# Two small weight loads moved onto the main load queue, and block diagonals built on VectorE instead of TensorE

## The chip, the cores and the metric

The kernel runs on one core of one Trainium2 chip. The metric is the device time of one execution in microseconds (us). Executions are in one of two states, fast or slow. The profile records one execution; its span is some 2 us shorter than the time quoted for the same execution.

Names used below: PE is TensorE, PEld its weight load, DVE is VectorE, ACT is ScalarE, POOL is GpSimd, SP is SyncE. SPq and ACTq are lines of the profile for the sequencers of SP and ACT issuing DMAs.

## The reference, cut to what matters

The function is a gated mix of a linear attention and a gated feed-forward block over 2048 tokens of width 640. The change touches only the front of the attention branch: the per-head 20x20 weights w_phi, and the vector gate_w.

```python
g  = sigmoid((x * gate_w).sum(-1, keepdims=True))
qkv = x @ wqkv                                   # 640 -> 3 * 640, 32 heads of 20
pq = einsum("bhsd,hdf->bhsf", q, w_phi)          # per head 20 x 20
pk = einsum("bhsd,hdf->bhsf", k, w_phi)
# softmaxes of +-pq and +-pk, linear attention, @ wo  -> a ; geglu ffn -> b
return g * a + (1 - g) * b
```

The kernel folds w_phi into the k and q weights: it multiplies a transposed weight matrix by a block diagonal matrix made of w_phi ("fold"). So the first fold needs two things, the block diagonals (`BD`) and the transposed k weights (`wkT`). gate_w becomes one more column behind the folded k weights (`w3[:, :, 2*D]`), so that one projection computes k and the gate together.

## The kernel before

The loads stand in this order. SP issues nearly everything; x of block 0 and the v weights come as plain loads, the rest of x and the k and q weights as transposing loads. ACT issues the two small loads.

```python
sc.dma("act", wphi_sb[20 partitions, (h f)] <- w_phi "h d f -> d h f")     # 25 KB, 640 pieces of 40 bytes
sc.dma("act", gw_row[1, 640] <- gate_w)                                    # one row
xload(0); xload(2)                                # SP: x of block 0, two halves
for kt in range(KD): vload(kt)                    # SP: v weights, five pieces
xblock(1)                                         # SP, transposing: x of block 1 -> xT
wload(wkT, D, "wkT"); wload(wqT, 0, "wqT")        # SP, transposing: k, then q weights
xblock(2); xblock(3)
# ... feed-forward weights ...
```

PE then makes the block diagonals and the gate column with ten small matmuls, and DVE masks them out of PSUM:

```python
# blockdiag(): five matmuls spread w_phi (20 partitions) over 128 partitions by a selection matrix,
# five 1x1 matmuls turn the gate row into a column; then, for i in 0..4:
DVE tensor_tensor: BD[:, i] = psum * mask[:, i]   # 0 outside the diagonal blocks
DVE tensor_copy:   w3[:, :, 2*D] = gate column
```

The order of work on PE at the front is:

```python
warm(7)                                  # matmuls on zeros while x is on its way
xt(0..3)                                 # 20 PE transposes of x of block 0
vs(...)                                  # v of token tiles 0..3, the block diagonals in between
self.v_early(4, 6); self.v_early(5, 0)   # v of tiles 4, 5: need x of block 1
f(0, "k", ...); f(1, "k", ...)           # folds: need BD and wkT
self.v_early(6, 6)
f(2, "k", ...); f(3, "k", ...); f(4, "k", ...)
...
```

The softmax here doesn't subtract the row's maximum and nothing guards it: scores larger than these inputs give would overflow.

## Time and profile before

| | |
|---|---|
| time, median (range of 6 runs) | 299.75 us (299.39 to 300.2) |
| span of the profiled run | 297.8 us |
| PE busy | 292.9 us, 98% |
| PE on the chain that ended last | 96% |

The page of the kernel before: its span; the busy time of each engine (us, share, number of instructions); and the chain that ended last, first by engine, then by source line.

```profile
span 297.8 us, 4821 instructions
...
PE 292.9 (98%) x1913; PEld 171.9 (58%) x1913; DVE 162.2 (54%) x318; ACT 104.3 (35%) x183; POOL 29.0 (10%) x58
...
PE 96%; DMA 1%; ACT 1%; issue 0%; SPq 0%; ACTq 0%
PE ps L616 37%; PE ps L694 20%; PE ps L359 13%; PE ps L700 7%; PE ps L504 7%; PE ps L649 4%; PE ps L452 3%; PE ps L368 2%; PE ps L626 1%; DMA xtok<-in_A_x_dram 1%; PE ps L339 1%; ACT Eq L510 1%; ACT Ek L418 0%; PE ps L284 0%; PE ps L304 0%
```

PE is busy 98% of the span and is 96% of the chain: whatever the change does, it shows only if it removes PE work or makes PE wait. Line L616 is the feed-forward matmul; nothing of the change is near it.

The front of the same execution, from the view of instructions in order of time. Columns: start in us, length in us, engine, source line, operation, output<-inputs, shape, count, and in brackets the idle time before it and what ended that.

```profile
4.19 3.83 SPq L229 DMA_TRANSPOSE xT<-in_A_x_dram  x1
...
4.40 0.73 PE L284 MATMUL ps<-ident,xtok 128*128 128x128 bf16 x10
...
5.45 0.73 PE L284 MATMUL ps<-ident,xtok 128*128 128x128 bf16 x10 [0.32 <-DMA xtok<-in_A_x_dram]
...
8.06 3.35 SPq L226 DMA_TRANSPOSE wkT<-in_A_wqkv_dram  x1
...
9.39 0.48 PE L304 MATMUL ps<-wphi_sb,esel 20*128 20x140 bf16 x5
...
9.71 0.26 PE L312 MATMUL ps<-one,gw_row 1*128 1x1 bf16 x5
...
12.10 2.88 PE L359 MATMUL ps<-w,xT 128*128 128x512 bf16 x20
...
14.99 0.80 PE L339 MATMUL ps<-BD,wkT 128*128 128x140 bf16 x12
```

Read it in two columns. PE: ten transposes of x at 4.40, a wait of 0.32 us for the second half of x, ten more at 5.45, the ten small matmuls at 9.39 and 9.71, v of tiles 4 and 5 at 12.10, and the first fold at 14.99. SP: the transposing load of x of block 1 is issued from 4.19 for 3.83 us, that of the k weights from 8.06 for 3.35 us. The trace has the last of the k weights landing at 14.95 us, and PE begins the fold at 14.99 without having idled.

### The profile page before, as it was taken

To read this page: it belongs to the slowest core of one execution; us is meant where nothing else is said; L and a number is where in the kernel's file an instruction comes from. 1 tells how busy PE (TensorE), PEld (TensorE's weight loads), DVE (VectorE), ACT (ScalarE), POOL (GpSimd) and SP (SyncE) were. 2 spreads that over 40 slices of the span, in tenths; PEclk is the share of its full clock that TensorE was granted. 3 is DMA by queue.
4 is the path that set the end of the run, shared out by engine and by line. 5 is a ranking of instruction groups with operands and counts; after the bars stand their busy time and mean duration, and the time that the engine had idled before them with its cause. 6 is when DMAs were issued, how large, how long until landed. Compare 5 with 4: busy or idle time off the path is not lost.

```text
span 297.8 us, 4821 instructions
## 1 busy us (share of the span) xinstructions
PE 292.9 (98%) x1913; PEld 171.9 (58%) x1913; DVE 162.2 (54%) x318; ACT 104.3 (35%) x183; POOL 29.0 (10%) x58
## 2 busy tenths in 40 slices
PE   7999999999999999999999999999999999999996
PEld 3576656555544556775555577655457765545763
DVE  1348999998875679514655700455580045567000
ACT  3367787576663221121222212122221212232111
POOL 7000000000000011201011100101110010111000
PEclk9999999999999999999999999999999999999999
DMA  7999990000002122112011200201101010110101
GB/s 219 211 209 335 355 350 18 0 0 2 0 2 53 35 20 28 47 44 66 3 22 22 20 27 24 60 6 25 22 9 37 22 46 23 22 24 0 44 24 44
DMA packets 38098, 18.77 MB, mean 63 GB/s; under 512 B 30203, under 2 KB 37820, under 8 KB 38076
## 3 DMA queue, kind: packets, MB, share of 16 engines
q1 hardware_dynamic: 37424, 18.44, 24.4%
q8 instruction: 15, 0.25, 0.3%
q10 hardware_dynamic: 652, 0.03, 0.1%
q14 instruction: 7, 0.06, 0.1%
HBM read 8.96 MB, written 2.62 MB: 39 GB/s over the span
## 4 chain that ended last, share of the span: by engine, by line
PE 96%; DMA 1%; ACT 1%; issue 0%; SPq 0%; ACTq 0%
PE ps L616 37%; PE ps L694 20%; PE ps L359 13%; PE ps L700 7%; PE ps L504 7%; PE ps L649 4%; PE ps L452 3%; PE ps L368 2%; PE ps L626 1%; DMA xtok<-in_A_x_dram 1%; PE ps L339 1%; ACT Eq L510 1%; ACT Ek L418 0%; PE ps L284 0%; PE ps L304 0%
## 5 line engine op out<-in xcount | busy, mean ns | idle before, releaser
L616 PE MATMUL ps<-xT,wu_sb 128*128 128x512 bf16 x260 | 64.6, 379 | 0.2 <-ACT Eq L510 0.2
L616 PE MATMUL ps<-xT,wg_sb 128*128 128x512 bf16 x260 | 64.6, 379 | 0.0
L694 PE MATMUL ps<-wd_sb,hT 128*128 128x320 bf16 (+2 forms) x448 | 63.6, 299 | 0.0
L621 DVE TENSOR_TENSOR hT<-ps,gl 128x512 bf16<-128x512 f32 x52 | 35.7, 688 | 44.5 <-PE ps L616 44.4
L619 ACT ACTIVATE gl<-ps 128x512 bf16<-128x512 f32 x52 | 31.1, 597 | 80.8 <-PE ps L616 78.6
L694 PEld LDWEIGHTS ps<-wd_sb,hT 128*128 128x128 bf16 x448 | 43.2, 98 | 17.8
L616 PEld LDWEIGHTS ps<-xT,wu_sb 128*128 128x128 bf16 x260 | 25.4, 98 | 31.1 <-issue 0.7
L359 PE MATMUL ps<-w,xT 128*128 128x512 bf16 (+3 forms) x240 | 40.9, 321 | 0.0
L616 PEld LDWEIGHTS ps<-xT,wg_sb 128*128 128x128 bf16 x260 | 25.0, 98 | 27.2
L710 ACT ACTIVATE outsb<-ps,Gm 128x640 bf16<-128x640 f32 (+2 forms) x17 | 13.0, 763 | 74.7 <-PE ps L700 74.7
L678 POOL TENSOR_TENSOR Og<-O,O 128x640 bf16<-128x640 bf16 x16 | 22.3, 1394 | 167.5 <-DVE O L676 167.5
L359 PEld LDWEIGHTS ps<-w,xT 128*128 128x128 bf16 x240 | 22.4, 97 | 18.2
L665 DVE RECIPROCAL RH<-ps 128x32 f32<-128x32 f32 x16 | 5.7, 358 | 40.7 <-PE ps L649 39.7
L429 DVE TENSOR_REDUCE Dk<-Ek 128x64 f32<-128x1280 bf16 x16 | 23.7, 1480 | 3.2 <-ACT gcol L421 3.2
L438 DVE TENSOR_TENSOR Ek<-Ek,Dk 128x640 bf16<-128x640 bf16 x32 | 25.0, 821 | 0.6
L504 PE MATMUL ps<-xT,wq 128*128 128x512 bf16 x100 | 24.7, 379 | 0.3 <-ACT Eq L510 0.3
L676 DVE TENSOR_TENSOR O<-ps,RH 128x640 bf16<-128x640 f32 x32 | 24.8, 816 | 0.0
L700 PE MATMUL ps<-wo_sb,goT 128*128 128x320 bf16 (+2 forms) x160 | 24.5, 299 | 0.0
L510 ACT ACTIVATE Eq<-ps 128x512 bf16<-128x512 f32 x40 | 21.7, 604 | 4.0 <-PE ps L504 4.0
L418 ACT ACTIVATE Ek<-ps 128x640 bf16<-128x640 f32 x32 | 20.7, 702 | 3.5 <-PE ps L359 3.5
L700 PEld LDWEIGHTS ps<-wo_sb,goT 128*128 128x128 bf16 x160 | 15.5, 98 | 6.3
L649 PEld LDWEIGHTS ps<-KV,Eq 128*128 128x128 bf16 x192 | 12.0, 98 | 3.1
(66 smaller groups left out, 154.2 us busy)
## 6 DMA issues: line engine op xcount, KB each, us to landing
out_dram<-outsb SPq DMA_DIRECT2D x15, 160.0 KB, 2.0
wd_sb<-in_B_w_down_dram SPq DMA_DIRECT2D x1, 2080.0 KB, 12.4
wg_sb<-in_B_w_gate_dram SPq DMA_DIRECT2D x1, 1120.0 KB, 5.7
wu_sb<-in_B_w_up_dram SPq DMA_DIRECT2D x1, 1120.0 KB, 9.6
wg_sb<-in_B_w_gate_dram SPq DMA_DIRECT2D x1, 960.0 KB, 9.9
wu_sb<-in_B_w_up_dram SPq DMA_DIRECT2D x1, 960.0 KB, 10.2
w<-in_A_wqkv_dram SPq DMA_DIRECT2D x5, 160.0 KB, 4.0
wo_sb<-in_A_wo_dram SPq DMA_DIRECT2D x1, 800.0 KB, 10.1
```

The lines of the kernel that those rows point to most:

```text
L359: sc.op("pe", lambda e, kt=kt: e.matmul(self.bank(bank)[:, bcol:bcol + n], self.xT[:, kt, t * P:(t + 1) * P], self.w3[:, kt, c0:c0 + n], s ...
L429: sc.op("dve", lambda e: e.tensor_reduce(self.Dk[:, se, 0, :].rearrange("p (s h) -> p s h", h=H), self.Ek[:, se, :, :].rearrange("p s (h d ...
L438: sc.op("dve", lambda e, v=v, r=r: e.tensor_tensor(v, v, r, ALU.mult), reads=[("Rk", se)], writes=[("Ek", se, s)])
L504: sc.op("pe", lambda e, kt=kt: e.matmul(self.bank(bank), self.wq2[:, kt, i * P:(i + 1) * P], self.xT[:, kt, b * self.BT:(b + 1) * self.BT] ...
L510: sc.op("act", lambda e, s=s, scale=scale: e.activation(self.Eq[:, s, i, b * self.BT:(b + 1) * self.BT], self.bank(bank), AF.Exp, scale=sc ...
L616: sc.op("pe", lambda e, kt=kt, w=w, bk=bk: e.matmul(self.bank(bk), w[:, kt, c * P:(c + 1) * P], xs(kt), start=(kt == 0), stop=(kt == self. ...
L619: sc.op("act", lambda e: e.activation(self.gl[:, slot, :], self.bank(banks[0]), AF.Gelu_apprx_tanh), reads=[("ps", banks[0])], writes=[("g ...
L621: sc.op("dve", lambda e: e.tensor_tensor(self.hT[:, c, :], self.bank(banks[1]), self.gl[:, slot, :], ALU.mult), reads=[("ps", banks[1]), ( ...
L649: sc.op("pe", lambda e, s=s, i=i, n=n, o0=o0, k0=k0, bk=bk, r=r: e.matmul(self.bank(bk)[:, o0:o0 + n], self.Eq[:, s, i, t * P:(t + 1) * P] ...
L676: dve(lambda e, o=o, f=f, s=s: e.tensor_tensor(o, V[s][:, :, :, 0:DH], f, ALU.mult), rb + [key(6 + s)], [("O", s, sl)], guard=old)
L694: sc.op("pe", lambda e: e.matmul(self.bank(bk, w), self.hT[:, c, tt * P:(tt + 1) * P], self.wd_sb[:, c, w0:w0 + w], start=(c == 0), stop=F ...
L700: sc.op("pe", lambda e: e.matmul(self.bank(bk, w), self.goT[:, gs, k, :], self.wo_sb[:, k, w0:w0 + w], start=False, stop=(k == self.KD - 1 ...
```

## The change

The intent is to free PE of ten small matmuls and to bring x in sooner. w_phi is loaded so that each of its 640 features stands on its own partition; the block diagonal is then one product of a broadcast and a mask. The gate weights are loaded straight into their column, one element per partition and row. Both loads now stand on SP behind v, and the second half of x of block 0 goes to ACT's queue.

```diff
+        xload("sp", 0)
+        xload("act", 2)
         for kt in range(KD):
             sc.dma("sp", ... self.w3[:, kt, 0:D] <- v weights ...)
-        sc.dma("act", ... self.wphi_sb[20 partitions] <- "h d f -> d h f" ...)
-        sc.dma("act", ... self.gw_row[0:1, :] <- gate_w ...)
-        xload(0); xload(2)                                        # both on SP
+        sc.dma("sp", lambda e: e.dma_start(
+            self.wphi_sb[:, :, :], self.wphi.rearrange("h d f -> (h d) f").rearrange("(i p) f -> p i f", p=P)), ...)
+        sc.dma("sp", lambda e: e.dma_start(
+            self.w3[:, :, 2 * D:2 * D + 1], self.gw.rearrange("(k p o) -> p k o", p=P, o=1),
+            allow_slow_non_contiguous=True), ...)
 ...
-    def blockdiag(self, banks):     # 10 matmuls, 5 products from PSUM, 1 copy
+    def blockdiag(self):
+        for i in range(self.KD):
+            n = self.HHI[i] - self.HLO[i] + 1
+            self.sc.op("dve", lambda e: e.tensor_tensor(
+                self.BD[:, i, 0:n * DH].rearrange("p (h d) -> p h d", d=DH),
+                self.wphi_sb[:, i, :].unsqueeze(1).to_broadcast([P, n, DH]),
+                self.mask[:, i, 0:n].unsqueeze(2).to_broadcast([P, n, DH]), ALU.mult), ...)
 ...
-        vs(0,0) vs(1,0) vs(2,0) vs(0,1) vs(3,0) vs(1,1) vs(2,1) vs(3,1)
+        for t in range(4): vs(t, 0)
+        for t in range(4): vs(t, 1)
```

More of the change, by code (lines that the diff above doesn't have):

```diff
@@ L156, in alloc @@
         self.zero = T("zero", [P, 512], BF16)
-        self.gw_row = T("gw_row", [1, D], BF16)
-        self.one = T("one", [1, 1], BF16)
         self.gcol = T("gcol", [P, NT], F32)
@@ L163, in alloc @@
         self.BD = T("BD", [P, KD, 8 * DH], BF16)
-        self.wphi_sb = T("wphi_sb", [DH, D], BF16)
-        self.esel = T("esel", [DH, 8, DH], BF16)
+        self.wphi_sb = T("wphi_sb", [P, KD, DH], BF16)
         def place(lists):
@@ L209, in loads, with xload @@
         x4 = self.x[0:self.BT, :].rearrange("(p j) n -> p j n", j=self.TB)
-        def xload(j):
-            sc.dma("sp", lambda e: e.dma_start(self.xtok[:, j:j + 2, :], x4[:, j:j + 2, :]),
+        def xload(q, j):
+            sc.dma(q, lambda e: e.dma_start(self.xtok[:, j:j + 2, :], x4[:, j:j + 2, :]),
                    writes=[("xtok", j), ("xtok", j + 1)])
-        def vload(kt):
+        xload("sp", 0)
+        xload("act", 2)
+        for kt in range(KD):
             sc.dma("sp", lambda e: e.dma_start(self.w3[:, kt, 0:D], w3[:, kt, 2 * D:3 * D]), writes=[("wv", kt)])
-        sc.dma("act", lambda e: e.dma_start(self.wphi_sb[:, :].rearrange("d (h f) -> d h f", f=DH),
-                                            self.wphi.rearrange("h d f -> d h f")), writes=["wphi"])
-        sc.dma("act", lambda e: e.dma_start(self.gw_row[0:1, :], self.gw.rearrange("(o n) -> o n", o=1)), writes=["gw_row"])
-        xload(0)
-        xload(2)
-        for kt in range(KD):
-            vload(kt)
+        sc.dma("sp", lambda e: e.dma_start(
+            self.wphi_sb[:, :, :], self.wphi.rearrange("h d f -> (h d) f").rearrange("(i p) f -> p i f", p=P)),
+            writes=["wphi"])
+        sc.dma("sp", lambda e: e.dma_start(
+            self.w3[:, :, 2 * D:2 * D + 1], self.gw.rearrange("(k p o) -> p k o", p=P, o=1),
+            allow_slow_non_contiguous=True), writes=["wgate"])
         def wload(T, c0, key):
@@ L257, in loads @@
                                        compare_op=ALU.not_equal, fill=1.0, base=0, channel_multiplier=1), ["ident"])
-        pool(lambda e: e.tensor_copy(
-            self.esel[:, :, :], self.ident[0:DH, 0:DH].unsqueeze(1).to_broadcast([DH, 8, DH])), ["esel"], reads=["ident"])
         for i in range(KD):
@@ L292, in x_transpose @@
             sc.op("dve", lambda e: e.tensor_copy(out, src), reads=[("ps", b)], writes=[("xT", t)])
-    def blockdiag(self, banks):
-        sc = self.sc
+    def blockdiag(self):
         DH = self.DH
-        es = self.esel[:, :, :].rearrange("d j f -> d (j f)")
-        plan = []
-        for bk, chunks in zip(banks, ((0, 1, 2), (3, 4))):
-            c = 0
-            for r, i in enumerate(chunks):
-                n = (self.HHI[i] - self.HLO[i] + 1) * DH
-                off = (P * i) % DH
-                sc.op("pe", lambda e, i=i, n=n, c=c, off=off, bk=bk, r=r: e.matmul(
-                    self.bank(bk)[:, c:c + n], es[:, off:off + P],
-                    self.wphi_sb[:, self.HLO[i] * DH:self.HLO[i] * DH + n], start=(r == 0), stop=(i in (2, 4)),
-                    skip_group_check=True),
-                    reads=["esel", "wphi"], writes=[("ps", bk)], signal=(i in (2, 4)))
-                plan.append((i, bk, c, n))
-                c += n
-        for kt in range(self.KD):
-            sc.op("pe", lambda e, kt=kt, c=c, bk=bk: e.matmul(
-                self.bank(bk)[:, c + kt:c + kt + 1], self.gw_row[0:1, kt * P:(kt + 1) * P], self.one[:, :],
-                start=False, stop=(kt == self.KD - 1), skip_group_check=True), reads=["gw_row", "one"],
-                writes=[("ps", bk)], signal=(kt == self.KD - 1))
-        for i, b, cc, n in plan:
-            sc.op("dve", lambda e, i=i, b=b, cc=cc, n=n: e.tensor_tensor(
-                self.BD[:, i, 0:n].rearrange("p (h d) -> p h d", d=DH),
-                self.bank(b)[:, cc:cc + n].rearrange("p (h d) -> p h d", d=DH),
-                self.mask[:, i, 0:n // DH].unsqueeze(2).to_broadcast([P, n // DH, DH]), ALU.mult),
-                reads=[("ps", b), ("mask", i)], writes=[("BD", i)])
-        sc.op("dve", lambda e: e.tensor_copy(
-            self.w3[:, :, 2 * self.D:2 * self.D + 1], self.bank(bk)[:, c:c + self.KD].unsqueeze(2)),
-            reads=[("ps", bk)], writes=["wgate"])
@@ L326, in fold @@
+        for i in range(self.KD):
[3 more added lines that the diff above has]
+                self.wphi_sb[:, i, :].unsqueeze(1).to_broadcast([P, n, DH]),
+                self.mask[:, i, 0:n].unsqueeze(2).to_broadcast([P, n, DH]), ALU.mult),
+                reads=["wphi", ("mask", i)], writes=[("BD", i)])
     def fold(self, kt, which, banks, ekey):
@@ L528, in attention_state @@
         sc.op("dve", lambda e: e.memset(self.zero[:, :], 0.0), writes=["zero"])
-        sc.op("dve", lambda e: e.memset(self.one[:, :], 1.0), writes=["one"])
         def warm(n):
@@ L540, in attention_state @@
         xt(3, 3, "a")
-        vs(0, 0)
-        vs(1, 0)
-        vs(2, 0)
-        vs(0, 1)
-        vs(3, 0)
-        vs(1, 1)
-        vs(2, 1)
-        vs(3, 1)
+        for t in range(4):
+            vs(t, 0)
+        for t in range(4):
+            vs(t, 1)
         for t in range(4):
             vs(t, 2)
-        self.blockdiag((6, 7))
         for t in range(4):
             vs(t, 3)
+        self.blockdiag()
         for t in range(4):
```

## The prediction

> **What bounds the kernel.** The page gives TensorE 292.9 us busy of a 297.8 us span (98%), and the chain of waits is PE for 96%. PE is idle for about 4.9 us: 1.26 us before the first warm-up matmul, about 2.7 us of output at the end, 0.3 us for the second half of x, 0.3 us for an exp. So only PE work removed, or a DMA landing moved where PE waits, can change the time, and the change touches only the first 15 us.
>
> There (timeline): x of block 0 is issued by SP at 0.80 and 1.25 us and lands after 3.5 and 4.1 us, near 4.35 and 5.4 us. After warm-up (4.38 us) ten transposes run, PE waits until 5.45, ten more end at 6.18, then the v steps. At 9.46 the block-diagonal and gate matmuls take 0.51 us of the chain (0.41 + 0.10). At 14.99 the first fold starts exactly when the transposing load of the k weights has landed (groups by tile: PEld waited 0.2 us for it).
>
> **What the change does.**
> - Removes ten small PE matmuls: -0.5 us on PE before the fold.
> - DVE: five products of 0.29 us, now from SBUF, about the same; one 0.17 us copy less. DVE is idle from 6.4 to 9.8 us: free.
> - x over two queues: the Trainium skill, "DMA: Bandwidth & Descriptors", section "Issuing engines are not separate DMA queues", says queues share the same 16 engines and only issue time is saved. The trace fits: 300 to 370 GB/s from 3 to 6 us with one queue. I expect the halves to land together near 4.7 to 5.0 us: the first 0.5 us later, the second 0.5 us earlier. The 20 transposes then run without a gap, and end near 6.2 to 6.4: 0 to +0.2 us.
> - SP's issue stream loses one x issue (0.43 us) and gains w_phi (0.61 us on ACT before, 640 pieces) and the gate column. The same page ("Rules for kernel authors") says a strided last dimension becomes one descriptor per element: 640 more pieces of 2 bytes; I estimate 0.6 us of issue as for w_phi. So the transposing load of x block 1 is issued near 4.9 instead of 4.19 us, and the k weights behind it (8.06) up to 0.75 us later. Transposing issues last 3.0 to 4.1 us, so less back-pressure may absorb a part.
>
> **On the critical path.** PE reaches the first fold 0.3 to 0.5 us earlier, but the k weights land 0.2 to 1.0 us later (15.2 to 16.0 instead of 14.95). The later one counts: the fold moves by about +0.5 us, and the saving on PE turns into a wait. After it PE is dense: the shift reaches the end.
>
> **Prediction.** 300.3 us, 8 in 10 between 299.4 and 301.5. Faster by over 2%: 0.01; within 2%: 0.98; slower by over 2%: 0.01. Slightly slower is likelier than slightly faster.
>
> **Right or wrong in the profile.** PE busy falls by about 0.5 to 1 us while the span doesn't; a PE wait of 0.5 to 1.5 us for the k weights appears before the first fold; SP issues x block 1's transposing load near 4.9 us; the 0.3 us wait between the transposes is gone, and one of 0.3 to 0.6 us stands before the first.
>
> **What would make it wrong.** The issue of the 2-byte column, or its read-modify-writes, takes several us and delays the transposing loads: slower by 2 to 3 us. Or the transposing load is limited by data in flight rather than by issue, and the k weights land as before: faster by 0.3 to 0.5 us.

## The result, and the profile after

| | before | after |
|---|---|---|
| time, median of 6 runs | 299.75 us | 301.35 us |
| range | 299.39 to 300.2 | 299.79 to 301.52 |
| span of the profiled run | 297.8 us | 299.3 us |
| first fold on PE begins | 14.99 us | 16.42 us |

The ratio of the times is 1.0044, 95% interval 1.0023 to 1.0066: slower by 0.4%, well inside 2%. Here and below a ratio is the mean time of one kernel's fast runs over that of the other's fast runs of the same rounds, so it is not quite the ratio of the medians quoted. One of the six runs after, at 299.79 us, stands apart from the other five (301.24 to 301.52).

The page after, the same lines:

```profile
span 299.3 us, 4795 instructions
...
PE 292.7 (98%) x1903; PEld 171.5 (57%) x1903; DVE 162.2 (54%) x316; ACT 104.2 (35%) x183; POOL 28.7 (10%) x57
...
PE 92%; DMA 3%; SPq 2%; ACT 1%; issue 0%; ACTq 0%
PE ps L584 37%; PE ps L662 20%; PE ps L332 12%; PE ps L668 7%; PE ps L477 7%; PE ps L617 4%; PE ps L425 3%; DMA wkT<-in_A_wqkv_dram 3%; PE ps L594 1%; SPq L226 1%; PE ps L312 1%; SPq L214 1%; ACT Eq L483 1%; ACT Ek L391 0%; SPq L218 0%
```

PE's share of the chain fell to 92% although PE does the same work but for ten tiny matmuls; "DMA wkT" has entered the chain with 3%.

The front of the execution after, in order of time, as shown of before:

```profile
3.75 0.43 SPq L215 DMA_DIRECT2D wphi_sb<-in_A_w_phi_dram  x1
...
4.23 0.53 SPq L218 DMA_DIRECT2D w<-in_gate_w_dram  x1
...
4.52 1.49 PE L279 MATMUL ps<-ident,xtok 128*128 128x128 bf16 x20
...
4.80 3.58 SPq L226 DMA_TRANSPOSE xT<-in_A_x_dram  x1
...
7.63 1.18 DVE L293 TENSOR_TENSOR BD<-wphi_sb,mask 128x140 bf16<-128x140 bf16 x5 [1.37 <-DMA wphi_sb<-in_A_w_phi_dram]
8.43 4.41 SPq L223 DMA_TRANSPOSE wkT<-in_A_wqkv_dram  x1
...
11.94 2.89 PE L332 MATMUL ps<-w,xT 128*128 128x512 bf16 x20 [0.28 <-DMA xT<-in_A_x_dram]
...
16.42 0.80 PE L312 MATMUL ps<-BD,wkT 128*128 128x140 bf16 x12 [1.59 <-DMA wkT<-in_A_wqkv_dram]
```

And the one new line in the view of waits (engine, line, what it waited for: us in total, times, longest):

```profile
PE ps L312 <- DMA wkT<-in_A_wqkv_dram: 1.6, 1, 1.6
```

PE no longer has the ten matmuls, and the 20 transposes run in one piece. PE is ready for the first fold at about 14.83 us, a little earlier than before (14.98), but the k weights land at 16.37 us and PE waits 1.59 us. The fold starts 1.43 us later than before, and the span is 1.5 us longer. From the first fold to the end of the span it is 282.82 us before and 282.89 us after. So nearly the whole loss exists by 16.4 us and is carried unchanged to the end.

The question is why the k weights land 1.42 us later. SP issues x of block 1 at 4.80 instead of 4.19 us, which is 0.6 of it at most.

### The profile page after: what moved, and what is told of

Same layout as the page of the kernel before. It is cut to its first block, busy times and chain, and to the rows that moved or that the text cites. A ratio compares the mean times of both kernels' runs of the same rounds, so it can differ in the third digit from the quotient of the medians.

```text
span 299.3 us, 4795 instructions
## 1 busy us (share of the span) xinstructions
PE 292.7 (98%) x1903; PEld 171.5 (57%) x1903; DVE 162.2 (54%) x316; ACT 104.2 (35%) x183; POOL 28.7 (10%) x57
## 4 chain that ended last, share of the span: by engine, by line
PE 92%; DMA 3%; SPq 2%; ACT 1%; issue 0%; ACTq 0%
PE ps L584 37%; PE ps L662 20%; PE ps L332 12%; PE ps L668 7%; PE ps L477 7%; PE ps L617 4%; PE ps L425 3%; DMA wkT<-in_A_wqkv_dram 3%; PE ps L594 1%; SPq L226 1%; PE ps L312 1%; SPq L214 1%; ACT Eq L483 1%; ACT Ek L391 0%; SPq L218 0%
```

## The experiments

Each kernel was timed in five rounds beside the kernel before, whose median was 299.94, 300.00 and 299.88 us in the three sets of four. All results were correct. In each set, one execution of each kernel was profiled.

**Theory 1, that of the prediction:** the transposing loads are late because SP issues them late. **Rivals:** the DMA engines are occupied by the small pieces, whoever issues them; x over two queues does harm; the new order of v steps does harm.

### 1. Both small loads issued by ACT

```diff
-        sc.dma("sp", ... wphi_sb ...)
-        sc.dma("sp", ... gate column ...)
+        sc.dma("act", ... wphi_sb ...)
+        sc.dma("act", ... gate column ...)
```

> The changed kernel with w_phi and the gate column issued by ACT behind the second half of x, in place of SP. Theory (the two issues on SP hold back the transposing loads): SP issues x of block 1 near 3.75 us instead of 4.80, the k weights land 1.0 to 1.5 us earlier than 16.4, the wait before the first fold falls from 1.6 to under 0.6 us, and the time is 299.3 to 300.0 us, 0.4 to 0.6% under the changed kernel. Rival (the pieces themselves occupy the 16 DMA engines, whoever issues them): the k weights still land near 16.4 us and the time stays near 301.3 us.

Measured: 301.54 us, ratio 1.0057 (1.0044 to 1.0070). From the view in order of time:

```profile
1.24 0.46 ACTq L215 DMA_DIRECT2D wphi_sb<-in_A_w_phi_dram  x1
...
1.73 0.55 ACTq L218 DMA_DIRECT2D w<-in_gate_w_dram  x1
...
3.62 5.72 SPq L226 DMA_TRANSPOSE xT<-in_A_x_dram  x1
...
9.39 3.63 SPq L223 DMA_TRANSPOSE wkT<-in_A_wqkv_dram  x1
...
16.70 0.80 PE L312 MATMUL ps<-BD,wkT 128*128 128x140 bf16 x12 [1.63 <-DMA wkT<-in_A_wqkv_dram]
```

SP issues x of block 1 at 3.62 us, earlier than in the kernel before, and it helps nothing: that issue now lasts 5.72 us, and PE waits 1.63 us for the k weights. Theory 1 falls. The start of an issue is not what counts.

The trace's landings show what an issue waits for. In all fourteen profiles the issue of x of block 1 ends 0.02 to 0.56 us after the last plain load ahead of it has landed (here 9.10 and 9.34 us; before 7.72 and 8.02; after 8.22 and 8.38), and that of the k weights 0.8 to 1.4 us after x of block 1 has landed wherever it follows directly. That is an observation; what holds the issue was not tested.

### 2. Only the gate column issued by ACT

```diff
-        sc.dma("sp", ... gate column ...)
+        sc.dma("act", ... gate column ...)
```

> The changed kernel with only the gate column (640 pieces of 2 bytes) issued by ACT; w_phi stays on SP. Theory: SP issues x of block 1 near 4.25 us, about half of the effect of moving both: 299.7 to 300.7 us. If the 2-byte column alone is the costly one, the time is that of moving both; if w_phi is, 301.3 us as in the changed kernel.

Measured: 300.88 us, ratio 1.0031 (1.0015 to 1.0046); PE waits 1.03 us for the k weights. The median is 0.2 us above the range of the expected half-effect (299.7 to 300.7 us), and the reason given for it fell with run 1. The packets tell more: from 4.5 to 5.5 us the trace has 335 packets of 2 bytes and 10 packets of v, where the kernel after moves 258 packets of v in that time. Pieces on ACT's queue thus displace v on SP's queue. This fits in part the Trainium skill, "DMA: Bandwidth & Descriptors", section "Queues, rings and completion order", by which each engine goes round the queues it has work for: the two queues do share the engines, but 335 records against 10 are no even turns, and no run here shows how the turns are counted.

### 3. The old order of the v steps

```diff
-        for t in range(4): vs(t, 0)
-        for t in range(4): vs(t, 1)
+        for t, kt in ((0, 0), (1, 0), (2, 0), (0, 1), (3, 0), (1, 1), (2, 1), (3, 1)): vs(t, kt)
```

> The changed kernel with the old order of the first eight v steps. Theory (only the landing of the k weights counts): the two short waits of 0.2 and 0.3 us of the weight loads for the fourth x tile go, the wait before the first fold grows by the same, the time stays within 0.1% of the changed kernel. Rival (the new order of the v steps costs the time): 0.3 to 0.5 us faster.

Measured: 301.01 us, ratio 1.0038 (1.0023 to 1.0053). The kernel after had 1.0044 in other rounds; the intervals overlap, and PE waits 1.15 us for the k weights in the profile. The wait did not grow as expected; in this profile the k weights land at 15.94 instead of 16.37 us, and PE's clock rose only at 6.50 us (4.97 after; see run 8). The order is not the cause; that it gives a tenth of a per cent can't be excluded.

### 4. The kernel before plus the two loads

```diff
 (the kernel before, all else unchanged)
+        sc.dma("sp", ... scr_phi <- w_phi, feature by feature ...)      # read by nobody
+        sc.dma("sp", ... scr_gate[:, :, 0:1] <- gate_w ...)             # read by nobody
         xblock(1)
```

> The kernel before, unchanged in all it computes, with two more loads on SP behind v: w_phi feature by feature and the gate column, into tiles that nobody reads. Theory: this alone makes the loss. SP issues x of block 1 about 1.0 us later (5.2 instead of 4.19), a wait of 1.0 to 2.1 us for the k weights appears before the first fold, and the time is 300.7 to 301.9 us. Rival (the loss comes from x over two queues or from the new block diagonals): 299.8 us as before.

Measured: 300.29 us, ratio 1.0016 (1.0003 to 1.0030).

```profile
5.23 3.41 SPq L237 DMA_TRANSPOSE xT<-in_A_x_dram  x1
...
8.69 3.23 SPq L234 DMA_TRANSPOSE wkT<-in_A_wqkv_dram  x1
...
15.52 0.80 PE L347 MATMUL ps<-BD,wkT 128*128 128x140 bf16 x12
```

The direction is as expected, the size is not: 0.35 us, where at least 0.9 was expected. The k weights landed 0.52 us later than before, not 1.4. In its profile PE itself only got to the fold at 15.52 us, probably because its clock rose late (6.62 us, before 4.19; PE was busy for 14.13 us ahead of the fold, before 13.38; see run 8), so a wait doesn't show there. This run is a miss of the size, and it is taken up at the end.

### 5. x over two queues alone

```diff
 (the kernel before)
-        sc.dma("act", w_phi) ; sc.dma("act", gate row) ; xload(0) ; xload(2)      # x on SP
+        xload("sp", 0) ; xload("act", 2) ; sc.dma("act", w_phi) ; sc.dma("act", gate row)
```

> The kernel before with one part of the change alone: the second half of x of block 0 goes to ACT's queue, ahead of the two small loads that ACT issued already; block diagonals on PE as before. Theory 2 (the k weights land a fixed time after all plain loads of the start have landed; what counts is how long those take, not when SP issues): the plain loads are the same, so v lands near 7.7 us as before, the k weights near 15 us, and the time is within 0.3 us of the kernel before, although SP issues x of block 1 0.45 us earlier. Rival 1 (SP's issue time counts): the k weights land 0.4 us earlier; PE is then free of waits, the time falls 0.0 to 0.3 us. Rival 2 (x over two queues is the harm): 300.7 us or more.

Measured: 299.83 us, ratio 0.9994 (0.9982 to 1.0006): no change.

```profile
3.70 4.47 SPq L229 DMA_TRANSPOSE xT<-in_A_x_dram  x1
...
8.22 3.04 SPq L226 DMA_TRANSPOSE wkT<-in_A_wqkv_dram  x1
...
14.96 0.80 PE L339 MATMUL ps<-BD,wkT 128*128 128x140 bf16 x12
```

SP issues x of block 1 at 3.70 instead of 4.19 us; the plain loads have landed at 7.86 us (before 7.72), the k weights at 14.91 us (before 14.95). That is theory 2 of the expectation: the plain loads ahead count, not the start of the issue. It also fits the statement of the Trainium skill quoted in the prediction, that queues share the DMA engines.

### 6. One PE block moved ahead of the first fold

```diff
+        self.v_early(6, 2)
         f(0, "k", ...) ; f(1, "k", ...)
-        self.v_early(6, 6)
         f(2, "k", ...) ; f(3, "k", ...) ; f(4, "k", ...)          # PSUM banks renamed to fit
```

> The changed kernel with one PE block (the v projection of token tile 6, 1.44 us) moved ahead of the first fold, PSUM banks renamed to fit. It moves no load. If the loss is PE's wait for the k weights alone, PE works through it: the wait falls from 1.6 to about 0.2 us and the time falls by 1.2 to 1.6 us under the changed kernel, to 299.7 to 300.1 us. If something later also lost time, less comes back.

Measured: 300.23 us, ratio 1.0009 (0.9996 to 1.0022), against 1.0044 of the kernel after. The two lines in order of time:

```profile
12.42 4.24 PE L332 MATMUL ps<-w,xT 128*128 128x512 bf16 x30
...
16.50 1.96 PE L312 MATMUL ps<-BD,wkT 128*128 128x140 bf16 x30
```

The k weights are late here too (15.91 us), and PE no longer waits for them. Of the expected 1.2 to 1.6 us, about 1.1 came back. So most of the loss is this wait; no load was touched.

### 7. The gate column behind the k weights

```diff
-        sc.dma("sp", ... self.w3[:, :, 2 * D:2 * D + 1] <- gate_w ...)
         xblock(1)
         wload(self.wkT, D, "wkT")
+        sc.dma("sp", ... self.gsm[:, :, 0:1] <- gate_w ...)      # a tile of its own
         wload(self.wqT, 0, "wqT")
 ...     (after the last k fold)
+        DVE tensor_copy: w3[:, :, 2*D] = gsm[:, :, 0]
```

> The changed kernel with the gate column's load issued by SP behind the k weights (into a tile of its own, copied by DVE), w_phi left behind v. Theory 2: the last plain load ahead of the transposing ones lands near 7.6 instead of 8.2 us, the k weights near 15.2 to 15.6 us, a wait of 0.4 to 0.9 us stays, the time is 300.0 to 300.6 us. Rival (the pieces cost the same wherever they stand): 301.3 us.

Measured: 299.06 us, ratio 0.9984 (0.9963 to 1.0004). Four of six runs are at 298.86 to 299.12, two at 300.02 and 301.02.

```profile
4.17 3.35 SPq L224 DMA_TRANSPOSE xT<-in_A_x_dram  x1
...
7.56 3.78 SPq L221 DMA_TRANSPOSE wkT<-in_A_wqkv_dram  x1
...
11.38 0.58 SPq L229 DMA_DIRECT2D gsm<-in_gate_w_dram  x1
12.02 4.59 SPq L221 DMA_TRANSPOSE wqT<-in_A_wqkv_dram  x1
...
13.95 0.79 PE L313 MATMUL ps<-BD,wkT 128*128 128x140 bf16 x12
```

The wait is gone. The last plain load ahead (w_phi) lands at 7.04 us, x of block 1 at 10.40 instead of 11.89, and the k weights at 13.34 instead of 16.37 us. That is 3.0 us earlier, where theory 2 expected 0.8 to 1.2. Half of it, 1.49 us, is there when x of block 1 lands. The other 1.5 us lie between the two transposing loads and needed another explanation. This run changes the column's place and its tile together; run 8 changes its place and keeps the tile.

### 8. Both small loads beside the transposing loads

```diff
-        sc.dma("sp", w_phi) ; sc.dma("sp", gate column)
+        (ACT, after its part of the transposes of x, once v has landed)
+        sc.dma("act", w_phi) ; sc.dma("act", gate column)
```

> The changed kernel with both small loads issued by ACT, but only when the last piece of v has landed (near 7.1 us), so that they run beside the transposing loads. Theory 2 with the transposing load waiting only for what stands ahead of it on its own queue: its issue ends near 7.4 us, x of block 1 lands near 10, the k weights near 14.5 to 15.0 us, no wait before the fold, time 299.1 to 299.6 us. If pieces on the other queue slow it as much as those ahead of it: 300.5 to 301.5 us.

Measured: 299.72 us, ratio 0.9988 (0.9976 to 1.0000). x of block 1 lands at 10.49 us, the k weights at 14.81 us, no wait for a load on PE.

```profile
3.62 4.48 SPq L220 DMA_TRANSPOSE xT<-in_A_x_dram  x1
...
8.15 3.72 SPq L217 DMA_TRANSPOSE wkT<-in_A_wqkv_dram  x1
8.26 0.68 ACTq L511 DMA_DIRECT2D w<-in_gate_w_dram  x1
...
14.87 0.79 PE L306 MATMUL ps<-BD,wkT 128*128 128x140 bf16 x12
```

The column goes into the same tile as in the kernel after, and issued by ACT as in runs 1 and 2, which were late; so what removes the wait is its place, not its tile or its queue. The k weights land as theory 2, with a wait only for the own queue, had them, x of block 1 half a microsecond later than it had (near 10); the time is just above the range given for that, 299.1 to 299.6. One likely reason can be read from the transposes of x, by tile (instruction group, count, shortest/median/longest in ns, first and last start in us), first in run 7, then in this run:

```profile
L280 PE MATMUL ps<-ident,xtok x20: 219/219/314, 4.3 to 5.5; 128*128 128x128 bf16 x20
```

```profile
L273 PE MATMUL ps<-ident,xtok x20: 286/311/311, 4.3 to 6.3; 128*128 128x128 bf16 x20
```

The same 20 transposes last 219 ns in the median in one profile and 311 in the other; v begins at 5.58 us there and at 6.45 us here. In the trace PE's clock goes to full at 4.70 us in run 7 and 6.95 us in this one; over the fourteen profiles it does so anywhere from 4.19 to 7.19 us. This fits the Trainium skill, "TensorE: Matmul & The Clock Gate", section "What's actually happening", which has the clock rise after a busy window of about 3.4 us that does not start with the kernel. The first PE work begins at 1.26 us in all of them. The varying moment agrees; but in two of the fourteen the clock rises less than 3.4 us after the first PE work (2.93 and 3.15 us), so the window need not be busy throughout. So the 0.87 us by which v begins later here go mostly with that phase, where PE is not waiting for data anyway. Whether the transposes themselves count as busy for the clock was not tested.

### 9. A load between the k and the q weights

Reading the packets of run 7 raised a suspicion. In eleven of the fourteen profiles one packet of 16 KB of the instruction queue (q8) stands on one DMA engine for about 1 us just as the k weights drain. In the view of DMA queues (packets, MB, share of 16 engines), from 14 to 15 us after:

```profile
q8 instruction: 1, 0.02, 7.2%
```

and from 14 to 15 us in run 7, where the k weights had landed by 13.34:

```profile
q8 instruction: 1, 0.02, 5.8%
```

This run adds a load where run 7 had one, and moves nothing.

```diff
 (the kernel after)
         wload(self.wkT, D, "wkT")
+        sc.dma("sp", ... self.gsm[:, :, 0:1] <- gate_w ...)      # once more, read by nobody
         wload(self.wqT, 0, "wqT")
```

> The changed kernel with nothing moved and one load added: the gate column once more, into a tile that nobody reads, between the transposing loads of the k and the q weights. Reading of the traces so far: in every kernel where the q weights follow directly, the k weights land 3.3 to 3.65 us after their issue ends, and a 16 KB instruction packet of about 1 us stands on one DMA engine at that moment; in the kernel with the gate column between them they landed after 2.0 us and the packet came later. If this place is what counts: the k weights land near 14.9 us, the wait falls from 1.6 to under 0.3 us, the time to 299.8 to 300.3 us. If only the pieces ahead of the transposing loads count: 301.3 us as in the changed kernel.

Run 8 did not fit this reading: there the q weights follow directly, but the k weights landed 2.95 us after their issue ended, and the packet came only at 15.74 us.

Measured: 301.38 us, ratio 1.0039 (1.0020 to 1.0058), and the wait is there:

```profile
PE ps L316 <- DMA wkT<-in_A_wqkv_dram: 1.8, 1, 1.8
```

So a load in that place does not help as such. But the 16 updates of the semaphore that tells of the k weights, taken for one per DMA engine, now show the fault alone (from the trace, us):

```
run 9:  14.52 14.54 14.55 14.56 14.58 14.59 14.60 14.62 14.63 14.64 14.66 14.67 14.68 14.70 14.71   16.43
        instruction packet 14.13 to 15.10
run 7:  13.18 13.19 13.20 13.20 13.22 13.23 13.25 13.25 13.26 13.26 13.27 13.27 13.27 13.28 13.28   13.34
        instruction packet 14.00 to 14.93
```

Fifteen engines have delivered at 14.71 us; the sixteenth does so 1.72 us later. In the kernels before, after, and runs 1, 4, 5 and 10 the last 4-byte record ahead of the landing, taken for the k weights' completion write, starts within 0.02 us of the end of the instruction packet (before: packet 12.89 to 13.85, record 13.84; after: 14.12 to 15.27, record 15.27). Runs 2, 3 and 6 have the packet and the late landings, but not such a record. In several profiles more than one update is late: eleven of the sixteen before (14.64 to 14.95 us), four after (16.06 to 16.37), so one held engine is not the whole account. In runs 7 and 11, where the k weights had landed before the packet started, they landed 2.0 us after the end of their issue; in the other profiles but run 8 it was 3.3 to 3.8 us. That the engine is the same one is inferred from these times; the records do not name it. What makes the packet start just then is open.

### 10. x back on one queue

```diff
 (the kernel after)
-        xload("act", 2)
+        xload("sp", 2)
```

> The changed kernel with the second half of x back on SP: the two small loads on SP and the new block diagonals alone. If the two queues of x do no harm (as x over two queues alone did none): the k weights land as late as in the changed kernel, near 16 us, and the time is 301.0 to 301.5 us. If the harm comes from both together (adding the two loads to the kernel before cost only 0.35 us): the k weights near 15.4 us and 300.2 to 300.6 us.

Measured: 301.09 us, ratio 1.0043 (1.0031 to 1.0055), as in the kernel after.

```profile
5.13 3.66 SPq L226 DMA_TRANSPOSE xT<-in_A_x_dram  x1
...
8.84 3.86 SPq L223 DMA_TRANSPOSE wkT<-in_A_wqkv_dram  x1
...
16.32 0.80 PE L312 MATMUL ps<-BD,wkT 128*128 128x140 bf16 x12 [1.66 <-DMA wkT<-in_A_wqkv_dram]
```

With run 5 this settles the two queues of x: they do neither harm nor good, alone or together with the rest.

### 11 and 12. Two candidates to beat both kernels

Run 11 is run 7 with the moved PE block of run 6 and the order of run 3.

> A candidate to beat both: gate column behind the k weights (own tile, DVE copy), the v block of tile 6 ahead of the first fold, the old order of the first eight v steps. Theory: no PE wait but for the start; 298.6 to 299.1 us, and fewer late runs than with the gate column moved alone, which had two of six above 300 us, because PE has 1.4 us more work before it needs the k weights.

Measured: 299.53 us (299.37 to 300.12), ratio 0.9993 (0.9981 to 1.0006). No wait for a load, no run above 300.2; but the median missed the expectation and is above that of run 7. In its profile v starts at 5.93 us against 5.58 in run 7, and its clock rose at 5.30 us against 4.70; whether its median is only that phase was not settled.

Run 12 also puts w_phi between x of block 1 and the k weights, and the block diagonals behind the first evacuations.

> As the first candidate, and w_phi too taken out of the way, between x of block 1 and the k weights, block diagonals on DVE after the first evacuations. Theory: x of block 1 lands 0.5 us earlier, near 9.9 us; the k weights are then not needed earlier, so the time is that of the first candidate, 298.6 to 299.1 us; slower if w_phi lands after 14 us and the block diagonals hold the fold.

Measured: 299.90 us, ratio 1.0003 (0.9988 to 1.0018). x of block 1 lands at 10.38 us, no earlier than in run 11. The k weights show the picture of run 9 again: fifteen landings by 14.65 us, the last at 16.43, with an instruction packet from 13.93 to 15.08; PE waits 0.60 us in spite of the moved block. Nothing is gained by moving w_phi.

### What the fourteen profiles say together

Landings of the profiled executions, in us from the start of the span; the time is the median of all runs of that kernel.

| kernel | gate column ahead of the transposing loads | last plain load ahead | x of block 1 | k weights | time |
|---|---|---|---|---|---|
| before | no | 7.72 | 10.46 | 14.95 | 299.75 |
| run 5 | no | 7.86 | 10.42 | 14.91 | 299.83 |
| run 7 | no | 7.04 | 10.40 | 13.34 | 299.06 |
| run 8 | no | 7.83 | 10.49 | 14.81 | 299.72 |
| run 11 | no | 7.34 | 10.31 | 13.56 | 299.53 |
| run 12 | no | 7.96 | 10.38 | 16.43 (w_phi ahead of it) | 299.90 |
| run 4 | yes, into a tile of its own | 8.50 | 10.86 | 15.47 | 300.29 |
| run 2 | yes, on ACT | 8.55 | 11.48 | 15.74 | 300.88 |
| after | yes | 8.22 | 11.89 | 16.37 | 301.35 |
| run 3 | yes | 8.78 | 11.65 | 15.94 | 301.01 |
| run 6 | yes | 8.80 | 11.63 | 15.91 | 300.23 (wait filled) |
| run 9 | yes | 8.21 | 11.73 | 16.43 | 301.38 |
| run 10 | yes | 8.65 | 11.73 | 16.28 | 301.09 |
| run 1 | yes, on ACT | 9.10 | 12.13 | 16.66 | 301.54 |

Without the column ahead, x of block 1 lands at 10.31 to 10.49 us in six profiles of six. With it, at 11.48 to 12.13 in seven of eight. Whether w_phi is ahead (runs 7, 11) or not (runs 8, 12) makes no difference. Run 4 is the exception: the same pieces ahead, but x of block 1 at 10.86 us.

The packets narrow it down. Behind the data of each of these loads stand 32 records of 4 bytes, taken for its completion writes. The last of them for x of block 1 starts at 9.12 to 9.88 us in the six profiles without the column ahead and at 10.03 to 10.94 us in all eight with it: before 9.62, run 4 10.07, after 10.03. It follows the last plain landing by 1.57 to 2.20 us in all fourteen, so theory 2 fits the data of x of block 1. Its landing comes 0.84 us after that record before, 0.78 us in run 4, but 1.86 us after, where eight of the sixteen updates come by 10.48 us and the other eight from 11.18 us on. So of the 1.43 us by which x of block 1 lands later after than before, 0.41 are later data, about what the same two loads cost in run 4 (0.45); the other 1.02 us lie between the last record and the landing, and no run explains them. Run 4 differs in where the column is written (rows 4 bytes apart instead of 2564) and in having w_phi early on ACT as well; which of these matters was not tried.

## Why the prediction was right or wrong

The measured 301.35 us is inside the range (299.4 to 301.5), close to its upper end, and the class "within 2%" is right. Point by point:

- **PE bounds the kernel and only PE work or PE waits count.** Right. The fold is 1.43 us later, the span 1.5 us longer, and all after the fold takes the same time.
- **The saving on PE turns into a wait for the k weights before the first fold.** Right, and confirmed by run 6, where filling the wait gives back about 1.1 us, and by run 7, where the load comes early and the wait is gone. The wait is 1.59 us; 0.5 to 1.5 was predicted.
- **"The k weights land 0.2 to 1.0 us later (15.2 to 16.0 instead of 14.95)."** This is the term that was mis-sized: +1.42 us, 16.37. The central 300.3 us carried +0.5 us for the fold; it was +1.43. The landing missed its own forecast; that the time still fell inside its range is partly luck, that of a range reaching 1.2 us above its centre.
- **Its reason, SP's issue stream, was wrong.** SP did issue x of block 1 at 4.80 us, as predicted near 4.9. But run 1 issues it at 3.62 us and the k weights land at 16.66; run 5 issues it 0.49 us earlier than before and the two landings come within 0.04 us of those before. What counts is the gate column's 640 pieces of 2 bytes ahead of the transposing loads: taking them out of the way (run 7) brings x of block 1 in 1.5 us earlier. How they do it is shown in part only: 0.41 us of the difference to the kernel before is later data, the rest is open (see the packets above). The prediction had named them as a risk ("2-byte column ... takes several us"), with 0.6 us of issue as its main estimate; their issue did last 0.53 us, and this was not their cost.
- **PE reaches the fold 0.3 to 0.5 us earlier.** It got there 0.15 us earlier (14.83 against 14.98): it also waited 0.28 us for x of block 1 at 11.94.
- **x over two queues lands together near 4.7 to 5.0 us, and PE waits 0.3 to 0.6 us before the first transpose.** The halves landed together, but at 4.29 and 4.47 us, and PE idled about 0.1 us. The estimate had left out that w_phi's pieces no longer ran beside x (1.80 to 4.06 us before, from 5.90 us after). For the time it makes no difference (runs 5 and 10).
- **DVE's part is free.** Right: five products of 0.30 us each, as before, at 7.63 us, with DVE idle again until 11 us.
- **PE busy falls by 0.5 to 1 us.** It fell from 292.9 to 292.7, all of it ahead of the fold (13.38 to 13.19 us; 279.55 us behind it in both). The ten instructions are gone, but the clock was full only from 4.97 instead of 4.19 us, and the transposes start about 107 ns apart before that moment and 56 ns apart after it. That probably took back the rest; it was not in the estimate.
- **What was not foreseen at all:** the instruction packet. By its times it delays the k weights in the kernel before too (landing 3.54 us after the end of the issue, 3.53 after), so it explains none of the difference between the two profiles, but 1.5 of the 3.0 us of run 7 go with it. That the one early run after (299.79), the two of run 9 (300.06 and 300.14) and the two late ones of run 7 are executions in which packet and load met the other way is argued, not shown: none of them was profiled.

Run 7 has the lowest median of all. Against the kernel before its interval (0.9963 to 1.0004) includes no gain; against the kernel after it was not timed in the same rounds, and their intervals against the kernel before do not overlap.

## What to carry to other kernels

Before moving a small load into the main queue, look at what stands behind it: here one load of 1.2 KB in 2-byte pieces, ahead of transposing loads on which PE waits, cost more than the ten matmuls saved (1.49 us at x of block 1, run 7 against after), and put behind or beside them it cost nothing that shows. The size does not carry over: added to the kernel before, the same pieces with w_phi cost 0.35 us (run 4). Where work and data arrive at the same instant, as at the first fold here, taking work away buys only a wait unless the data comes earlier too. To learn whether a load is late because of its issue or because of what is ahead of it, issue it earlier with the same bytes ahead (runs 1 and 5): a start that moves without the landing moving is the answer.

## What the Trainium skill lacked or had wrong

- "DMA: Bandwidth & Descriptors", section "Rules for kernel authors": that a strided last dimension becomes one descriptor per element agrees with the trace (640 packets of 2 bytes). It does not say what such a load does to a transposing load behind it: x of block 1 landed at 11.5 to 12.1 us instead of 10.3 to 10.5 in seven of eight profiles, 10.86 in the eighth.
- The same page, section "Issuing engines are not separate DMA queues": agrees (x over two queues: ratio 0.9994). What no page gives is how long the issue of a transposing load lasts behind plain loads: it started at 3.62 us and lasted 5.72 us in run 1, started at 4.80 and lasted 3.58 after, and ended 0.02 to 0.56 us after the last plain load had landed in every profile.
- "Runtime: NRT & Kernel Launch", section "Instruction fetch mechanics", has instructions come by DMA in blocks of 16 KiB and calls the cost mostly hidden. Here a 16384-byte packet at the front lasted 0.88 to 1.17 us, and in run 9 the k weights, with fifteen of sixteen updates in by 14.71 us, were complete at 16.43 us; that the packet caused this is inferred from the times.
- "TensorE: Matmul & The Clock Gate", "What's actually happening", gives the change of clock a spread of plus or minus 500 ns. Over the fourteen profiles, with the first PE work always at 1.26 us, it ranged from 4.19 to 7.19 us. The same page's "Part 4: PE-mode transpose" says the full clock does not engage for transposes, which do not count as busy in the same way. Here they ran at it once it was there: they start about 107 ns apart before the clock record shows full speed and 56 ns apart after it. Whether they help to bring it on was not tested.
- No page says how long a transposing load takes from the end of its issue to its landing: 2.0 us for the k weights in runs 7 and 11, which had landed before the instruction packet, 2.95 us in run 8, where the packet came later too but the two small loads ran beside them, and 3.3 to 3.8 us in the other eleven profiles.
